# Joining 64-bit weights: the sign carried by ScalarE's slope instead of by a VectorE operation

## The chip, the cores and the metric

The kernel runs on one core of a Trainium2 chip. The metric is device time in microseconds (us), the median of three runs. Engines are named as the profile names them: PE is TensorE's matmul and PEld its weight load, DVE is VectorE, ACT is ScalarE, POOL is GpSimd, SP is the queue that issues most of the DMAs.

## The reference, cut to what matters

```python
# 8 x 8 heads of 576 tokens x 64; linear attention with two softmaxes
kv  = einsum('bhsd,bhse->bhde', softmax_over_tokens(k), v)
x   = einsum('bhsd,bhde->bhse', softmax_over_features(q), kv)   # 4608 tokens x 512
xn  = x / sqrt(mean(x * x) + 1e-6) * rms_g
x2  = (silu(xn @ w_gate) * (xn @ w_val)) @ w_out                # 512 -> 1536 -> 512
h   = maximum(maximum(x2 @ w1, x2 @ w2), x2 @ w3)               # 512 -> 768
out = h @ w2_out                                                # 768 -> 512
```

All weight matrices (`w_gate`, `w_val`, `w_out`, and `w1`, `w2`, `w3`, `w2_out` of the second layer) reach the chip as 64-bit floating-point numbers, seen as pairs of 32-bit words: a lower word and an upper word, alternating in memory.

## The kernel before, in words

The tokens are worked on in nine groups of 512 (`g` = 0 to 8). For each group the first layer runs over twelve blocks `f` of 128 hidden features. An iteration (g, f) multiplies the group's x by a gate block (12 matmuls into bank `pg`, L523 to L525), by a value block (12 into `pv`), forms tanh on ACT (L698), two products on DVE (L699, L710), splits the result into a high and a low part (L713 on ACT, L717 on DVE) and adds the block before it into the output (12 matmuls into `acc`, L529 to L531). There is one bank `pg`: L699 is its last reader, and the first matmul of the next iteration's gate product waits for it. Every matrix is held as a high and a low part of reduced width, so that each product takes three matmuls.

While group g is multiplied, the attention of group g + 1 is done between its iterations, in four pairs of heads: `k_max`, `k_exp`, `make_kv` (ten matmuls `pk`, L368), `make_x` (`px`) and so on. For group 1 (and 0) q is transposed on PE (`pt`, L388).

The weights of the first layer are built during group 0 alone, block f + 1 while block f is multiplied, in two halves of 768 columns (class `Weights`). One half goes through: load both words (SP), `scale` (L150: ACT multiplies the upper word, read as a 32-bit float, by 2^-112 into `y`), `join` (L155 to L157, three operations on DVE), `high` (L168, ACT) and `low` (L173, DVE). Block 0 and block 1 are built ahead of the first iterations, while the attention of group 0 is still running; group 0's scale `rstd` is found by a chain of small DVE operations (L458 to L474), goes through PE (L483) and ACT (L485), and is needed by `u` (L696), which for the first two blocks reads `pg` in place of L698 and L699.

The weights of the second layer are built during groups 1 to 7 (class `Ahead`), 24 pieces of 512 columns: load (SP), `join` (L213 on ACT, L214 to L216 on DVE, in place in tile `st`), sums (L228 to L231), and `quarter`, which splits on ACT and POOL and stores to memory. They are first read in group 8. From about 960 us on the second layer runs, and none of the joins is left.

No order of instructions is written out by hand. The framework places each engine's instructions in a queue by itself, from the order of the program and its own estimate of when operands will be there; each engine then works its queue strictly in that order. `tc.issue_after` ties a few helpers behind one instruction. In group 0 the joins of the two halves of a block stand mixed with the small operations of other chains on DVE, as the rows below show.

What a join before does, on integers: upper word scaled (its exponent field shrinks from 11 to 8 bits), shifted left by 3, then the sign taken from the original upper word, then the top 3 bits of the lower word put in at the bottom.

Of the kernel before, what the change touches and what calls it, by code (L numbers as in the profile page):

```python
# [8 lines left out]
F32 = mybir.dt.float32  # L9
F32R = mybir.dt.float32r  # L10
I32 = mybir.dt.int32
AF = mybir.ActivationFunctionType
ALU = mybir.AluOpType
# [34 lines left out]
def attention_moe_moe(ctx: ExitStack, tc: tile.TileContext, q, qt, k, kt, v, w1, rms_g, w2, w2_out, out):  # L48
# [14 lines left out]
    nc = tc.nc  # L63
# [60 lines left out]
    class Weights:  # L124
# [18 lines left out]
        def scale(self, f, h):  # L143
            if f in JOINED_IN:
                if h == 0:
                    self.place = wpool.tile([P, 2, HALF], F32, tag=JOINED_IN[f], name=f"y_{f}")
                self.y[f, h] = self.place[:, h, :]
            else:
                self.y[f, h] = two.tile([P, HALF], F32, tag="st", name=f"y_{f}_{h}")
            nc.scalar.activation(self.y[f, h], self.words[f, h][1].bitcast(F32), AF.Copy, scale=2.0**-112)  # L150

        def join(self, f, h):
            low, high = self.words.pop((f, h))
            y = self.y[f, h].bitcast(I32)
            nc.vector.tensor_scalar(y, y, 3, None, op0=ALU.logical_shift_left)  # L155
            nc.vector.scalar_tensor_tensor(y, high, -(2**31), y, op0=ALU.bitwise_and, op1=ALU.bitwise_or)
            nc.vector.scalar_tensor_tensor(y, low, 29, y, op0=ALU.logical_shift_right, op1=ALU.bitwise_or)  # L157

        def half(self, half, f, h):
            key = (1, f)  # L160
# [21 lines left out]
    class Ahead:  # L182
# [27 lines left out]

        def join(self, i):
            low, high = self.st[i]
            nc.scalar.activation(high.bitcast(F32), high.bitcast(F32), AF.Copy, scale=2.0**-112)  # L213
            nc.vector.tensor_scalar(low, low, 29, None, op0=ALU.logical_shift_right)  # L214
            nc.vector.scalar_tensor_tensor(low, high, -(2**31), low, op0=ALU.bitwise_and, op1=ALU.bitwise_or)
            nc.vector.scalar_tensor_tensor(high, high, 3, low, op0=ALU.logical_shift_left, op1=ALU.bitwise_or)  # L216

        def places(self, u):
# [314 lines left out]
    def evacuate(pt, dst, name, m, scale):  # L533
        pool, tag, bufs = ((two, "y", 3), (two, "y", 3), (two, "y", 3), (one, "sacc", 1))[m]
        e = pool.tile([P, N], F32, tag=tag, name=f"{name}_{m}", bufs=bufs)
        nc.scalar.activation(e, pt, AF.Copy, scale=scale)
        nc.scalar.dma_start(dst, e)
# [538 lines left out]
```

## Time and profile before

| | before |
|---|---|
| median of 3 runs | 1540.95 us (1540.77 to 1541.8) |
| profiled execution, its own time | 1538.84 us |
| span of the profile | 1537.0 us |
| PE busy | 1503.1 us (98%) |
| DVE busy | 939.8 us (61%) |
| ACT busy | 578.4 us (38%) |
| POOL busy | 259.1 us (17%) |
| mean granted clock of TensorE | 0.995 of full speed |

The span runs from the first to the last instruction; the profiled execution's own time is 1.84 us longer. Busy shares are means over stages that differ: group 0 lies between about 24 and 160 us, groups 1 to 8 end near 960 us, and the second layer takes the rest.

### The profile page before, as it was taken

What the parts mean: (1) busy time and instruction counts of PE and PEld (TensorE: products, weight loads), DVE (VectorE), ACT (ScalarE), POOL (GpSimd) and SP (SyncE); (2) the same over time, 40 slices, a digit from 0 to 9 for tenths busy, and PEclk for the clock granted to TensorE, in tenths of its full rate; (3) what the DMA queues carried; (4) which work ended last, traced back from release to release, by engine and by line L of the source; (5) the groups of instructions that cost most, each with busy time, mean ns of one, the idle gap of its engine ahead of it and who ended that gap; (6) DMA issues with size and microseconds to landing.
All of it is one profiled execution on the core that took longest, in us unless ns stands there. A gap on an engine that the chain in (4) does not pass through costs nothing.

```text
span 1537.0 us, 19169 instructions
## 1 busy us (share of the span) xinstructions
PE 1503.1 (98%) x6790; PEld 1238.1 (81%) x6790; DVE 939.8 (61%) x1622; ACT 578.4 (38%) x1107; POOL 259.1 (17%) x307
## 2 busy tenths in 40 slices
PE   5899999999999999999999999999999999999999
PEld 4678778888888888888888888888888888888887
DVE  6999655556655657655563244438838838847722
ACT  6764443433444434334433231323413413413311
POOL 0000222331331422312403200011111111111100
PEclk9999999999999999999999999999999999999999
DMA  8842552651652644626505113055485485485573
GB/s 274 324 157 73 166 136 94 172 149 57 195 163 68 192 135 130 176 91 181 172 29 171 49 55 124 0 181 209 163 315 207 170 321 199 168 299 198 171 265 104
DMA packets 126062, 250.00 MB, mean 163 GB/s; under 512 B 26640, under 2 KB 51216, under 8 KB 125968
## 3 DMA queue, kind: packets, MB, share of 16 engines
q1 hardware_dynamic: 119056, 236.21, 47.5%
q10 hardware_dynamic: 6912, 12.59, 2.2%
q8 instruction: 53, 0.87, 0.2%
q14 instruction: 41, 0.34, 0.1%
HBM read 205.52 MB, written 43.22 MB: 162 GB/s over the span
## 4 chain that ended last, share of the span: by engine, by line
PE 84%; DVE 8%; DMA 3%; issue 2%; POOL 1%; ACT 1%; SPq 0%; POOLq 0%; ACTq 0%; DVEq 0%
PE pg L523 6%; PE pg L525 5%; PE pg L524 5%; PE acc L529 5%; PE acc L530 5%; PE acc L531 5%; PE pv L523 5%; PE pv L524 5%; PE pv L525 5%; PE p_a L531 4%; PE p_a L530 4%; PE p_a L529 4%; PE p_G L529 2%; PE p_G L531 2%; PE p_G L530 2%; PE pk L368 2%
## 5 line engine op out<-in xcount | busy, mean ns | idle before, releaser
L699 DVE SCALAR_TENSOR_TENSOR t<-t,pg 128x512 f32<-128x512 f32 x106 | 72.3, 682 | 112.2 <-ACT t L698 110.3
L801 POOL TENSOR_TENSOR temps_wl<-temps_wh 128x512 f32<-128x512 f32 x36 | 48.2, 1338 | 438.2 <-ACT temps_wh L800 363.5
L713 ACT CAST hh<-t 128x512 fp32r<-128x512 f32 x108 | 66.9, 619 | 121.9 <-DVE t L710 121.1
L717 DVE TENSOR_TENSOR hl<-t,hh 128x512 fp32r<-128x512 f32 x108 | 77.4, 717 | 56.1 <-ACT hh L713 55.4
L710 DVE TENSOR_TENSOR t<-t,pv 128x512 f32<-128x512 f32 x108 | 73.9, 685 | 43.4 <-PE pv L525 40.0
L698 ACT ACTIVATE t<-pg 128x512 f32<-128x512 f32 x106 | 62.7, 591 | 88.6 <-PE pg L525 87.2
L529 PE MATMUL p_a<-x_wh,chunk 128*128 128x512 f32 x240 | 93.4, 389 | 0.0
L531 PE MATMUL p_a<-x_wh,chunk 128*128 128x512 f32 x240 | 93.4, 389 | 0.0
L530 PE MATMUL p_a<-x_wl,chunk 128*128 128x512 f32 x236 | 91.8, 389 | 0.0
L236 POOL TENSOR_TENSOR wq<-st,wq 128x256 fp32r<-128x256 f32 x84 | 64.2, 779 | 39.0 <-ACT wq L235 34.3
L336 POOL TENSOR_TENSOR q<-q,qm 128x512 f32<-128x512 f32 x28 | 30.3, 1083 | 209.7 <-DVE qm L326 178.5
L796 ACT COPY temps_wh<-p_G 128x512 f32<-128x512 f32 x36 | 21.1, 586 | 104.5 <-PE p_G L531 104.2
L310 POOL TENSOR_TENSOR qT<-qT,stat 128x512 f32<-128x512 f32 x28 | 37.5, 1340 | 132.3 <-DMA stat<-stats 132.3
L93 DVE TENSOR_TENSOR ql<-qT,qh 128x512 fp32r<-128x512 f32 x24 | 18.5, 770 | 58.6 <-ACT qh L92 58.3
L427 POOL TENSOR_TENSOR sacc<-sacc,sq 128x512 f32<-128x512 f32 x21 | 27.4, 1303 | 159.3 <-ACT sq L426 135.6
L529 PEld LDWEIGHTS p_a<-x_wh,chunk 128*128 128x128 f32 x240 | 45.1, 188 | 9.3
L531 PEld LDWEIGHTS p_a<-x_wh,chunk 128*128 128x128 f32 x240 | 45.1, 188 | 9.3
L530 PEld LDWEIGHTS p_a<-x_wl,chunk 128*128 128x128 f32 x236 | 44.3, 188 | 9.2
L529 PE MATMUL p_G<-x_wh,chunk 128*128 128x512 f32 x123 | 48.2, 392 | 0.2
L531 PE MATMUL p_G<-x_wh,chunk 128*128 128x512 f32 x123 | 47.9, 389 | 0.0
L337 ACT ACTIVATE q<-q 128x512 f32<-128x512 f32 x28 | 17.7, 632 | 75.1 <-POOL q L336 67.4
L798 DVE TENSOR_TENSOR temps_wh<-temps_wh,p_V 128x512 f32<-128x512 f32 x36 | 24.6, 683 | 33.4 <-PE p_V L531 33.4
(689 smaller groups left out, 4523.3 us busy)
## 6 DMA issues: line engine op xcount, KB each, us to landing
chunk<-w_dram SPq DMA_DIRECT2D x112, 768.0 KB, 4.4
w_dram<-wq SPq DMA_DIRECT2D x84, 256.0 KB, 3.0
words<-in_w SPq DMA_DIRECT2D x24, 768.0 KB, 7.9
stat<-stats SPq DMA_DIRECT2D x112, 128.0 KB, 3.2
chunk<-w_dram SPq DMA_DIRECT2D x48, 256.0 KB, 3.6
k<-in_k SPq DMA_DIRECT2D x30, 320.0 KB, 4.0
v<-in_v SPq DMA_DIRECT2D x30, 320.0 KB, 4.5
st<-in_w SPq DMA_DIRECT2D x18, 512.0 KB, 4.8
```

Of the source, the lines that this page charges most:

```text
L236: nc.gpsimd.tensor_sub(t[:, 1, :], src, t[:, 0, :].bitcast(F32))
L523: nc.tensor.matmul(pt, hi[:, j, s], xhs[kk], start=(kk == 0), stop=False)
L524: nc.tensor.matmul(pt, hi[:, j, s], xls[kk], start=False, stop=False)
L525: nc.tensor.matmul(pt, lo[:, j, s], xhs[kk], start=False, stop=(kk == 3))
L529: nc.tensor.matmul(pt, ah, bh, start=first, stop=False, skip_group_check=onto)
L530: nc.tensor.matmul(pt, ah, bl, start=False, stop=False, skip_group_check=onto)
L531: nc.tensor.matmul(pt, al, bh, start=False, stop=last, skip_group_check=onto)
L698: nc.scalar.activation(t, pg, AF.Tanh, scale=0.5)
L699: nc.vector.scalar_tensor_tensor(t, t, 1.0, pg, op0=ALU.add, op1=ALU.mult)
L710: nc.vector.tensor_mul(t, t, pv)
L713: nc.scalar.copy(hh[g, f], t)
L717: lows.append(nc.vector.tensor_sub(hl[g, f], t, hh[g, f].bitcast(F32)))
```

## The change: what it does

ACT's scaling becomes a parametric ReLU: positive values are multiplied by 2^-112 as before, negative ones by 2^-112 times 2^32. For a negative word the factor of 2^32 adds 32 to the exponent field, which sets a bit that the shift left by 3 moves into the place of the sign. So the DVE operation that put the sign back is left out in both classes. In `Weights.join` the shift that stood alone now works on the lower word, in place, and the shift of `y` moves into the last operation; in `Ahead.join` the two operations that are left are the same as before.

```diff
-            nc.scalar.activation(self.y[f, h], self.words[f, h][1].bitcast(F32), AF.Copy, scale=2.0**-112)
+            nc.scalar.activation(self.y[f, h], self.words[f, h][1].bitcast(F32), AF.Prelu, scale=2.0**-112, alpha=2.0**32)
 
         def join(self, f, h):
-            low, high = self.words.pop((f, h))
+            low, _ = self.words.pop((f, h))
             y = self.y[f, h].bitcast(I32)
-            nc.vector.tensor_scalar(y, y, 3, None, op0=ALU.logical_shift_left)
-            nc.vector.scalar_tensor_tensor(y, high, -(2**31), y, op0=ALU.bitwise_and, op1=ALU.bitwise_or)
-            nc.vector.scalar_tensor_tensor(y, low, 29, y, op0=ALU.logical_shift_right, op1=ALU.bitwise_or)
+            nc.vector.tensor_scalar(low, low, 29, None, op0=ALU.logical_shift_right)
+            nc.vector.scalar_tensor_tensor(y, y, 3, low, op0=ALU.logical_shift_left, op1=ALU.bitwise_or)
...
         def join(self, i):
             low, high = self.st[i]
-            nc.scalar.activation(high.bitcast(F32), high.bitcast(F32), AF.Copy, scale=2.0**-112)
+            nc.scalar.activation(high.bitcast(F32), high.bitcast(F32), AF.Prelu, scale=2.0**-112, alpha=2.0**32)
             nc.vector.tensor_scalar(low, low, 29, None, op0=ALU.logical_shift_right)
-            nc.vector.scalar_tensor_tensor(low, high, -(2**31), low, op0=ALU.bitwise_and, op1=ALU.bitwise_or)
             nc.vector.scalar_tensor_tensor(high, high, 3, low, op0=ALU.logical_shift_left, op1=ALU.bitwise_or)
```

## Rows read from the trace of the kernel before

**Rows 1.** Page, part 1: busy us of each engine, share of span, instructions.
```profile
PE 1503.1 (98%) x6790; PEld 1238.1 (81%) x6790; DVE 939.8 (61%) x1622; ACT 578.4 (38%) x1107; POOL 259.1 (17%) x307
```

**Rows 2.** Windows: stretch, length, busy us (instructions) per engine, TensorE clock, DMA share, GB/s.
```profile
24.00:52.00 28.00, 18.34 (x81) 12.59 (x81) 25.02 (x54) 19.31 (x42) 0.00 (x0) 0.81 0.78 284
52.00:112.00 60.00, 59.59 (x268) 47.31 (x269) 58.92 (x101) 41.47 (x98) 0.62 (x6) 0.98 0.63 218
112.00:152.00 40.00, 39.28 (x181) 31.69 (x180) 39.59 (x70) 19.18 (x28) 0.20 (x2) 1.00 0.22 64
...
164.00:310.00 146.00, 141.53 (x647) 115.45 (x646) 84.28 (x159) 58.65 (x110) 39.92 (x49) 1.00 0.49 143
310.00:840.00 530.00, 529.77 (x2440) 440.36 (x2439) 310.13 (x576) 215.99 (x404) 145.68 (x175) 1.00 0.47 138
```

**Rows 3.** PE timeline, 29 to 52 us: start, length, instruction, [idle before it, releaser].
```profile
30.23 2.52 PE L368 MATMUL pk<-wh,wh 128*128 128x129 f32 x10 [0.35 <-DVE kv_raw L378]
...
48.52 1.11 PE L483 MATMUL rstd<-ident,z 128*128 128x128 f32 x4 [5.59 <-DVE z L474]
```

**Rows 4.** DVE timeline, 23 to 52 us.
```profile
25.66 0.96 DVE L156 SCALAR_TENSOR_TENSOR y<-words,y 128x768 int32<-128x768 int32 x1
...
41.65 0.95 DVE L156 SCALAR_TENSOR_TENSOR y<-words,y 128x768 int32<-128x768 int32 x1
...
48.39 0.95 DVE L156 SCALAR_TENSOR_TENSOR y<-words,y 128x768 int32<-128x768 int32 x1
49.26 1.81 DVE L157 SCALAR_TENSOR_TENSOR y<-words,y 128x768 int32<-128x768 int32 x2
50.99 0.68 DVE L696 TENSOR_TENSOR u<-pg,z 128x512 f32<-128x512 f32 x1
```

**Rows 5.** Waits of PE, whole span: who waited for whom, us in total, times, longest.
```profile
PE pg L523 <- DVE t L699: 2.6, 6, 0.8
```

**Rows 6.** DVE groups by form: count, busy us, mean ns of one, idle before.
```profile
L156 DVE SCALAR_TENSOR_TENSOR y<-words,y 128x768 int32<-128x768 int32 x24 | 22.7, 951 | 0.1
...
L215 DVE SCALAR_TENSOR_TENSOR st<-st 128x512 int32<-128x512 int32 x24 | 18.1, 755 | 2.6 <-ACT st L213 1.7 <-DVE ks L372 0.4
...
L155 DVE TENSOR_SCALAR y<-y 128x768 int32<-128x768 int32 x24 | 13.1, 552 | 0.7 <-ACT y L150 0.6
L214 DVE TENSOR_SCALAR st<-st 128x512 int32<-128x512 int32 x24 | 10.1, 423 | 22.6 <-DMA st<-in_w 19.7 <-DMA st<-in_w_out 2.9
...
L495 DVE TENSOR_SCALAR z<-var 128x512 int32<-128x512 int32 x7 | 3.0, 424 | 9.7 <-ACT var L493 9.7
```

**Rows 7.** ACT groups by form: count, busy us, mean ns of one, idle before.
```profile
L698 ACT ACTIVATE t<-pg 128x512 f32<-128x512 f32 x106 | 62.7, 591 | 88.6 <-PE pg L525 87.2 <-DVE hl L717 1.3
...
L150 ACT ACTIVATE y<-words 128x768 f32<-128x768 f32 x24 | 21.2, 907 | 3.9 <-DMA words<-in_w 2.2 <-DVE wl_(1, 4)_825 L173 0.8 <-DVE wl_(1, 10)_1348 L173 0.7
...
L420 ACT COPY xraw<-px 128x512 f32<-128x512 f32 x32 | 18.7, 585 | 16.4 <-PE px L410 8.2 <-PE px L404 7.2 <-PE px L406 0.8
...
L333 ACT ACT_TABLE_LOAD x1 | 1.3, 1283 | 4.8 <-DMA q<-in_q 4.8
...
L416 ACT ACTIVATE xraw<-px,gain 128x512 f32<-128x512 f32 x4 | 2.7, 683 | 4.3 <-PE px L406 4.3
```

**Rows 8.** PE timeline in group 0: transposes and `pk` of pairs two and four.
```profile
81.27 0.60 PE L388 MATMUL pt<-ident,q 128*128 128x128 f32 x4
81.70 1.28 PE L368 MATMUL pk<-v,k 128*128 128x129 f32 x10
...
121.70 1.28 PE L368 MATMUL pk<-v,k 128*128 128x129 f32 x10
```

**Rows 9.** Chain that ended last, group 2: start, us, what.
```profile
324.28 1.11 PE pk L368 x10
342.58 1.11 PE pk L368 x10
```

**Rows 10.** DVE timeline, 301 to 308 us, ahead of a late L699.
```profile
304.54 1.67 DVE L216 SCALAR_TENSOR_TENSOR st<-st 128x512 int32<-128x512 int32 x1
```

## The prediction, written before the changed kernel was run

> **What bounds the kernel now.** The page's busy shares come first [rows 1]: PE is busy for 98% of the span and DVE for 61%. Read alone, that says that DVE's time is worth nothing. The windows [rows 2] say where this fails. From 310 us to 840 us PE is busy for 529.77 of 530 us, so there nothing on another engine matters. Between 24 and 152 us, the stretch in which the first layer's weights are joined, DVE is busy for 25.02 + 58.92 + 39.59 = 123.5 of 128 us. There DVE is the full engine, and from 24 to 52 us PE is busy for only 18.34 of 28 us, at a mean granted clock of 0.81, so partly at the lower of TensorE's two levels (1.2 and 2.4 GHz). From 164 to 310 us PE misses 146 - 141.53 = 4.5 us.
>
> The PE timeline shows the largest pause of all [rows 3]: 5.59 us before the matmul of L483, which waits for the last L474, the end of the small chain that finds group 0's scale. The DVE timeline shows what that chain stands behind [rows 4]: joins are queued between its small steps, among them L156. After it comes `u` (L696), at 50.99 us, again behind an L156 and two L157. The waits of PE add one thing for later [rows 5]: the gate product waited for L699 six times, 2.6 us in all.
>
> **The change part by part.** *Removed.* 24 L156, 951 ns each, 22.7 us, and 24 L215, 755 ns each, 18.1 us, both on DVE [rows 6]. In a full queue one costs less than its length, since the next starts before it ends: L156 at 48.39, L157 at 49.26, so 0.87 us [rows 4]. DVE's busy time should fall from 939.8 to about 899 us.
>
> *Rewritten.* L155 now works on the lower word, which lies with a gap of one word. No row has that at 768 columns. L214 does it at 512 in 423 ns and L155 takes 552 ns without gaps [rows 6]; 423 + 256 x (552 - 423)/256 is the same 552, so I take no change. The bounds are 423 ns from below and the 951 ns of a two-operand form from above, that is -3 to +10 us of DVE time in all. It also no longer waits for ACT, because it reads the lower word alone. The last operation keeps its form and inputs of the same kind, so 951 ns.
>
> *ACT.* No row has a parametric ReLU. L150 takes 907 ns with a plain copy. From PSUM, a tanh (L698) takes 591 ns where a copy (L420) takes 585 ns, and a copy whose scale is read from memory (L416) takes 683 ns [rows 7]. So a join costs ACT between 0 and 98 ns more; nothing in the rows gives a gain. I take 6 ns, the change of function alone, since slope and scale are constants: 48 x 6 = 0.3 us, at most 48 x 98 = 4.7 us of ACT, of which only the few joins on the chain reach the end. ACT is busy for 80 of the 128 us between 24 and 152 us [rows 2]; if it had no room, that 2.4 us (24 x 98 ns) would be lost.
>
> The profile holds one table load on ACT, 1283 ns, though exp, tanh, square and copy all run [rows 7]. The Trainium skill, "ScalarE: Activation LUTs", section "Table sets: the hidden batching unit", says that functions are loaded in named sets, that relu, copy, identity and abs are in every set, and that a switch costs about 2.66 us; parametric ReLU is not in its list. The load of 1283 ns agrees with the page's own figure; no row shows whether parametric ReLU is in the set that is loaded. If it is, the sum below stands; if not, the last rival's does.
>
> *Term A, 24 to 52 us.* The chain here passes through L156 five times, but not all of that comes back. The first joins stand beside a PE at the low clock: `pk` at 30.23 waited 0.35 us for DVE [rows 3], so I give this part 0.4 us. The chain behind it has three L156 left: at 41.65, one of the same kind at 47.45, and at 48.39 [rows 4]. Two delay L474 and so L483, the third, with the L157 behind it, delays `u`. 3 x 0.87 = 2.6. A = 0.4 + 2.6 = 3.0 us. At least the two in front of L483 come back, 1.7 us; at most the five of the chain, and L155 leaving the chain once, 5 x 0.87 + 0.55 = 4.9 us.
>
> *Term B, 52 to 152 us.* 18 L156 fall here, 15.7 us of DVE, but PE is already nearly full, so only PE's losses can come back. Two measures of these. Matmuls per time: 530 us hold 2440 later on, 0.217 us each; 268 and 181 of them would take 58.2 and 39.3 us and take 60 and 40, a loss of 2.5 us [rows 2]. Time per pair: in group 0 from 81.70 to 121.70, 20.0 us, of which four transposes take 0.43 [rows 8]; in group 2 it takes 18.30 [rows 9]. So a pair loses 20.0 - 0.43 - 18.30 = 1.27 us, and 100 us lose 6.4. The truth is between, since the matmuls differ in kind. What is late next is PE itself, at its own pace. DVE keeps 58.92 + 39.59 - 15.7 = 82.8 of 100 us, so the greater part should return: B = 3.5 us, with 1 and 6.4 as ends. Low clock (0.98 here) makes up some: 0.02 x 60 = 1.2 us, and comes back only if the pause before it becomes short enough.
>
> *Term C, 152 us on.* Of the six waits for L699, four have L215 and L216 directly ahead of it in DVE's queue (the one at 304.54 stands for them [rows 10]). Each loses one operation of about 0.6 us from start to start, and no wait was longer than 0.8 us. 4 x 0.6 = 2.4; two waits are themselves shorter than 0.6 us, so C = 2.2 us, from 0.5 to 3. From 310 us on the joins are hidden under PE; after 840 us nothing changes. No DMA moves to another place; a tile comes free earlier by the operation left out, and the words' next load starts that much earlier, into a DMA share of 0.63 and 0.22 [rows 2].
>
> Sum: 3.0 + 3.5 + 2.2 = 8.7 us. The profiled execution took 1538.84 us (span 1537.0 and 1.84 around it), so 1530.1; its own span would be 1528.3. The median of the runs lies 2.1 us above the profiled execution, which gives **1532.2 us**.
>
> **The rivals.**
>
> *PE is the bound and takes nothing.* DVE's saved time becomes idle time, because the framework plans its queue anew with shorter joins and puts other work into the gaps. For it: PE is at 98%, and the losses in B are spread thin. Against it: three L156 lie plainly on the chain before 52 us. Then only A's lower end is left, or less: a gain of 0 to 3 us, say 1539.5 us.
>
> *The new queue order puts joins in front of L699.* The queue's order is the framework's, and what is ahead of L699 when the gate product has ended makes PE wait. At 304.54 L216 takes 1.67 us and L699 can only follow [rows 10]; it goes away with L215 only if the two do not meet elsewhere. Now there are six such waits in 28 pair boundaries of groups 1 to 7. At 0.8 us each, the longest of them [rows 5], A and B (6.5 us) are eaten when 8 more boundaries wait; from 12 more on the kernel is slower by over 0.2%. With 16 more, the time is 1540.95 - 6.5 + 12.8 = 1547 us. Against it: 22 of 28 boundaries already hold with more joins in the queue.
>
> *Parametric ReLU is not in the loaded set.* Then each join swaps the table twice, 2 x 1.283 = 2.57 us of ACT [rows 7]. In group 0, 24 joins add 62 us to ACT's 80 in a stretch of 128: ACT becomes the bound and the stretch grows by at least 14 us. The later 24 would each hold L698 for up to 2.57 us; at 1 us on PE each, 24 more. 1541 + 38 = 1579 us. This is the skill's rule named above, priced from rows. For it there is no row; against it, that four functions share one load.
>
> **How the numbers follow.** Forecast 0.75 (its own range 1527 to 1538), the first rival 0.16, the second 0.06, the last 0.03. What a measurement of this kernel can tell from no change is about 0.2%, 3.1 us. The forecast's low end is the sum of the upper ends, 4.9 + 6.4 + 3 = 14.3 us: 1526.7. Its high end with A, B and C at their lower ends, 3.2 us, is 1537.7, just outside no change. The range runs from 1527 to 1541, into the first rival, and leaves out the others. Faster 0.75, within 0.2% 0.16, slower 0.09.
>
> **What would show it.** In the changed profile L156 and L215 are gone, DVE's busy time is near 899 us, L150 stays within 0.91 to 1.01 us, and there is one table load. The pause before L483 is about 3.9 us instead of 5.59, `u` starts near 48 us, the last `pk` of group 0 comes 5 to 7 us earlier than 121.70, and DVE is clearly below nine tenths from 52 to 152 us. In group 1 the waits of PE for L699 fall from 2.6 to below 1 us. The forecast is wrong if `u` starts at 50 us or later, if group 0 ends less than 3 us earlier, if the waits for L699 in groups 1 to 7 grow, or if more than one table load appears.

## The result, and the profile after

The changed kernel takes **1526.43 us** (median of four runs, 1524.64 to 1528.49) beside 1541.38 us for the kernel before in the same session: ratio 0.9903, interval 0.9886 to 0.9920. A repeat in a later session gives 1530.51 beside 1543.13 us, ratio 0.9914 (0.9897 to 0.9931). So it is faster by 0.9%, between 12.6 and 15 us. The profiled execution took 1528.49 us against 1538.84 before, 10.35 us less; its span is 1526.3 us.

The page, part 1, of the kernel after: busy us, share of the span, instructions.
```profile
PE 1502.8 (98%) x6790; PEld 1241.5 (81%) x6790; DVE 907.8 (59%) x1574; ACT 578.5 (38%) x1107; POOL 259.6 (17%) x307
```
Against [rows 1] DVE has 48 instructions less and 32.0 us less, not the 41 us forecast. PE has the same work and, but for 0.3 us, the same busy time: the shorter span comes from PE standing still for 23.5 us instead of 33.9.

The groups by form, on DVE and ACT (count, busy us, mean ns of one, idle before). In the kernel after, L155 shifts the lower word, L156 is the last operation of the first layer's join, L213 and L214 are the second layer's two; from there on line numbers are lower by one or two than before.
```profile
L156 DVE SCALAR_TENSOR_TENSOR y<-y,words 128x768 int32<-128x768 int32 x24 | 22.7, 948 | 0.9 <-ACT y L150 0.8
L155 DVE TENSOR_SCALAR words<-words 128x768 int32<-128x768 int32 x24 | 13.1, 556 | 0.2
...
L214 DVE SCALAR_TENSOR_TENSOR st<-st 128x512 int32<-128x512 int32 x24 | 18.5, 773 | 3.1 <-ACT st L212 2.5
L213 DVE TENSOR_SCALAR st<-st 128x512 int32<-128x512 int32 x24 | 10.2, 424 | 22.4 <-DMA st<-in_w 19.1 <-DMA st<-in_w_out 3.3
```
```profile
L150 ACT ACTIVATE y<-words 128x768 f32<-128x768 f32 x24 | 21.4, 912 | 2.4 <-issue 1.2 <-DVE wl_(1, 5)_922 L172 0.6 <-DVE wl_(1, 10)_1326 L172 0.5
...
L331 ACT ACT_TABLE_LOAD x1 | 1.3, 1283 | 4.5 <-DMA q<-in_q 4.5
```
The shift of the gapped lower word costs 556 ns where the shift without gaps took 552, the parametric ReLU 912 ns where the copy took 907 [rows 6, 7], and there is still one table load.

The windows of the kernel after (stretch, length, busy us and instructions per engine, TensorE clock, DMA share, GB/s); after them one stretch of the kernel before.
```profile
24.00:52.00 28.00, 24.00 (x90) 18.23 (x89) 21.29 (x49) 19.11 (x42) 0.00 (x0) 0.70 0.74 273
52.00:112.00 60.00, 58.90 (x278) 47.96 (x277) 58.93 (x104) 45.98 (x105) 0.62 (x6) 1.00 0.65 234
112.00:152.00 40.00, 40.00 (x189) 33.08 (x188) 34.07 (x65) 19.84 (x29) 0.21 (x2) 1.00 0.23 71
152.00:290.00 138.00, 137.68 (x631) 113.43 (x630) 76.98 (x144) 56.08 (x106) 38.37 (x47) 1.00 0.50 148
...
310.00:840.00 530.00, 530.00 (x2447) 440.45 (x2446) 298.48 (x551) 214.51 (x400) 143.89 (x171) 1.00 0.46 135
```
```profile
152.00:290.00 138.00, 133.78 (x610) 109.05 (x609) 81.71 (x153) 56.55 (x106) 34.99 (x45) 1.00 0.47 139
```
Read the instruction counts, not the busy shares alone. From 52 to 112 us PE is busy for less than in [rows 2] (58.90 against 59.59 us) and does ten matmuls more, at a granted clock of 1.00 instead of 0.98. DVE stays full there (58.93 of 60 us), because joins of later blocks move into this stretch: it holds 13 last operations of a join (L156) and 14 subtractions (L172), where before it held ten of each (L157, L173). The largest difference stands where the forecast had put the least: from 152 to 290 us PE is busy for 137.68 instead of 133.78 us.

PE's timeline around the matmul of group 0's scale (start, length, instruction, idle before it), and below it the pair that answers to 121.70 in [rows 8].
```profile
44.87 0.39 PE L523 MATMUL pv<-raws,wl_(1, 0)_455 128*128 128x512 f32 x1
45.31 0.65 PE L481 MATMUL rstd<-ident,z 128*128 128x128 f32 x4
46.64 0.32 PE L355 MATMUL pb<-ident,km 128*128 128x128 f32 x1 [0.68 <-ACT z L483]
48.12 0.64 PE L521 MATMUL pg<-raws,wh_(1, 1)_523 128*128 128x512 f32 x1 [1.16 <-DVE u L694]
...
116.50 1.28 PE L366 MATMUL pk<-v,k 128*128 128x129 f32 x10
```
DVE's timeline ahead of it, and below it two rows of the kernel before, in which the chain that finds the scale reads its sums (L458, L456 after) and ends (L474, L472 after):
```profile
36.48 0.95 DVE L156 SCALAR_TENSOR_TENSOR y<-y,words 128x768 int32<-128x768 int32 x1
...
41.99 0.83 DVE L456 TENSOR_SCALAR var<-pv 128x1 f32<-128x1 f32 x4 [3.27 <-PE pv L442]
...
45.10 0.16 DVE L472 SCALAR_TENSOR_TENSOR z<-a,z 128x4 f32<-128x4 f32 x1
45.18 0.55 DVE L155 TENSOR_SCALAR words<-words 128x768 int32<-128x768 int32 x1
45.65 1.82 DVE L172 TENSOR_TENSOR wl_(1, 1)_545<-y,wh_(1, 1)_523 128x768 fp32r<-128x768 f32 x2
47.38 0.68 DVE L694 TENSOR_TENSOR u<-pg,z 128x512 f32<-128x512 f32 x1
```
```profile
40.45 0.35 DVE L458 TENSOR_SCALAR var<-pv 128x1 f32<-128x1 f32 x4
...
48.31 0.15 DVE L474 SCALAR_TENSOR_TENSOR z<-a,z 128x4 f32<-128x4 f32 x1
```
The 5.59 us pause of [rows 3] is gone, but only 3.2 us of that is the scale's matmul coming earlier (45.31 instead of 48.52). The rest is that the gate and value matmuls of block 0, which before had ended at 42.9 us, now run until 45.3. The chain itself has a new order: it begins 1.5 us later than before and takes 3.1 us from its first row to its last instead of 7.9, because the joins that stood between its steps [rows 4] now stand ahead of it or behind it. `u` starts at 47.38 instead of 50.99 [rows 4], with one shift and two subtractions between it and the scale, and no L156. Group 0's last `pk` comes 5.20 us earlier.

The waits of PE after, from 24 to 152 us, and below them all that it waited for from 152 to 290 us; the third fence is that last stretch of the kernel before (who waited for whom, us in total, times, longest).
```profile
PE pg L521 <- DVE u L694: 1.2, 1, 1.2
PE pg L521 <- ACT wh_(1, 3)_717 L167: 1.1, 1, 1.1
...
```
```profile
PE pg L521 <- DVE t L697: 0.2, 1, 0.2
```
```profile
PE pg L523 <- DVE t L699: 2.1, 4, 0.8
PE px L408 <- ACT kvh L92: 2.1, 2, 1.4
```
Up to 152 us the change brings one new wait, 1.1 us for block 3's upper half, and `u` still holds up 1.2 us. From 152 us on, before, the four waits of [rows 5] that fall into this stretch take 2.1 us, and the two for `kvh` another 2.1. After, 0.2 us are left of it all.

Two marks divide the rest: the `pk` of a pair at the start of group 1's stretch (mark 1) and the one four pairs later (mark 2), here before and then after.
```profile
174.34 1.28 PE L368 MATMUL pk<-v,k 128*128 128x129 f32 x10
287.04 1.27 PE L368 MATMUL pk<-v,k 128*128 128x129 f32 x10
```
```profile
169.07 1.27 PE L366 MATMUL pk<-v,k 128*128 128x129 f32 x10
276.71 1.28 PE L366 MATMUL pk<-v,k 128*128 128x129 f32 x10
```
From mark 1 to mark 2 it is 112.70 us before and 107.64 after. By these marks the profiled executions differ as follows: 3.61 us up to `u`, 1.59 more up to group 0's last `pk`, 0.07 more to mark 1, 5.06 in group 1, and 0.4 behind it (the last matmul starts at 1532.95 and at 1522.23).

### The profile page after: what moved, and what is told of

Its sections match the earlier page's. It is cut to its first block, busy times and chain, and to the rows that moved or that the text cites. A ratio compares the mean times of both kernels' runs of the same rounds, so it can differ in the third digit from the quotient of the medians.

```text
span 1526.3 us, 19104 instructions
## 1 busy us (share of the span) xinstructions
PE 1502.8 (98%) x6790; PEld 1241.5 (81%) x6790; DVE 907.8 (59%) x1574; ACT 578.5 (38%) x1107; POOL 259.6 (17%) x307
## 4 chain that ended last, share of the span: by engine, by line
PE 94%; DVE 2%; ACT 1%; DMA 1%; POOL 1%; issue 1%; SPq 0%; POOLq 0%; ACTq 0%; DVEq 0%
PE pg L521 7%; PE pg L523 6%; PE pg L522 6%; PE acc L527 6%; PE pv L523 6%; PE acc L528 6%; PE pv L521 6%; PE pv L522 6%; PE acc L529 6%; PE p_a L528 4%; PE p_a L527 4%; PE p_a L529 4%; PE p_G L527 2%; PE p_G L528 2%; PE p_G L529 2%; PE pk L366 2%
## 5 line engine op out<-in xcount | busy, mean ns | idle before, releaser
L335 ACT ACTIVATE q<-q 128x512 f32<-128x512 f32 x28 | 17.7, 633 | 76.8 <-POOL q L334 70.9
L233 ACT CAST wq<-st 128x256 fp32r<-128x256 f32 x84 | 33.6, 418 | 32.1 <-DMA w_dram<-wq 17.1
```

## The experiments

Each was timed in five rounds against the kernel before. "Stretch" is the time from mark 1 to mark 2.

**The change again.** No edit.

> The changed kernel once more, for the interval and for a second profile. Theory 'clock': the 4.2 us by which its median lies closer to a gain of 15 us than its profiled execution does (10.35 us) is TensorE at its lower clock between 24 and 52 us in some executions and not in others; then executions of the changed kernel differ by 2 to 4 us, the longer ones have the lower mean clock, and a profile of a short one (about 1524.5 us) shows a granted clock near 0.9 or more in 24 to 52 us where the first profile shows 0.70. Rival 'constant offset': every execution takes the same time up to 0.5 us, and the profile is only slower by its recording; then the new profile shows 0.70 there again and the times stay apart.

Measured: 1530.51 us, ratio 0.9914. The repeat's profile has `u` 2.16 us earlier than before, mark 1 3.93, mark 2 9.57 and the last matmul 8.28 us. So the parts repeat: the start gives 2 to 4 us, group 1 gives 5 to 6. What is behind mark 2 doesn't: 0.4 us more was won there, 1.3 us are given back here. Runs of the same kernel differ: before took 1538.14 to 1548.20 us over these sessions, and the six runs of this repeat 1525.19 to 1532.18, so the rival of a constant offset falls. Whether the clock makes the difference stays open: the execution that was profiled was the longest of the six (granted clock 0.76 from 24 to 52 us), and no short one was.

**The first layer's joins alone.**
```diff
 class Weights:   # scale: Prelu, join: two operations, as in the change
 class Ahead:     # scale: Copy, join: three operations, as before
```


> Only the first layer's weights are joined in the new way; the second layer's joins stay as before. Theory 'operations': terms A and B come with it and C does not: about 5.3 us less in the profile (3.6 up to u and 1.7 up to the last pk of group 0), and PE's waits in group 1 stay at 2 us or more. Rival 'order': the gain of group 1 comes from a queue order that group 0's shorter work brings about; then about 10 us less, with POOL's q subtraction of group 1 no longer behind the weight splits.

Measured: 1532.92 us, ratio 0.9937 (0.9921 to 0.9953). That is the size that the rival had given (about 10 us), not the theory's 5.3, and the stretch is 108.48 us. What the rival named as the reason isn't there, though: POOL's subtraction for q (L335, at 171.44 us) still stands behind weight splits.

**The second layer's joins alone.** The same edit the other way round.

> Only the second layer's weights are joined in the new way. Theory 'operations': term C alone, 2.2 us as predicted, up to the 5.4 us that the profile of the changed kernel shows after 152 us; nothing before 152 us. Rival 'order': 0 to 2 us, and the pause of PE near 183 us, behind POOL's weight splits, stays.

Measured: 1540.67 us, ratio 0.9984 (0.9975 to 0.9993). The parts are 9.7 and 2.5 us by ratio, together 12.2 beside 13.3 for the whole in the same session. The second layer's part is what term C gave it, but it isn't where C put it: its stretch is 112.40 us, as before, although L215 is gone; with L215 kept and the first layer's joins new it is 108.48 us. One profile of this kernel doesn't show where its 2.5 us lie. A place that fits is the time behind mark 2, which [rows 5] make look empty. From 290 us on PE waits for DVE and ACT for nothing in this profile; in the nine profiles of kernels that keep L215 it waits 0.5 to 3.7 us (0.5 in the kernel before), in the five of kernels without it 0 to 2.1 us. The two ranges overlap, so this isn't shown.

**The steeper slope alone.** The scaling as in the change; every operation of VectorE is kept.
```diff
-nc.scalar.activation(..., AF.Copy, scale=2.0**-112)
+nc.scalar.activation(..., AF.Prelu, scale=2.0**-112, alpha=2.0**32)
```


> ACT's parametric ReLU in both places, and all VectorE operations as before (the sign is then put in twice, which changes nothing). Theory: no change, within 1 us, L150 at 0.91 us, one table load, the same order on every queue. Rival: the framework's estimate of the new function differs and so does its order; then several us either way with the same busy times.

Measured: 1544.07 us, ratio 1.0005 (0.9995 to 1.0015). L150 takes 903 ns here, and there is one table load:
```profile
L333 ACT ACT_TABLE_LOAD x1 | 1.3, 1283 | 4.7 <-DMA q<-in_q 4.7
```
The function costs nothing that this run can tell from none, and the rival of the swapped tables falls. The Trainium skill, "ScalarE: Activation LUTs", section "Table sets: the hidden batching unit", doesn't list parametric ReLU among what every set holds; this trace shows it running beside exp and tanh under one load.

**Blocks 0 to 2 alone, and blocks 3 to 11 alone.** The change made for a part of the first layer's blocks; the second layer as before.
```diff
+if f <= 2:      # in the other kernel: f >= 3
+    Prelu, two operations
+else:
+    Copy, three operations
```


> New join for blocks 0 to 2 of the first layer only; blocks 3 to 11 and the second layer as before. It separates term A. Theory 'backlog' (DVE falls behind in group 0, its late joins run into group 1's first q chain, and the 5 us of group 1 come from their being done earlier): u 3.0 to 3.6 us earlier, but the backlog is only shifted, so block 11 is still joined near 150 us, the second layer's first two pieces are still loaded after the last join, and PE's waits in group 1 stay; 3 to 4 us in all. Rival 'start' (a start earlier by 3 us is what moves group 1): 8 us or more in all.

> New join for blocks 3 to 11 of the first layer only. Theory 'backlog': u where it was before, block 11 joined near 130 us, the second layer's first loads 20 us earlier, PE's waits in group 1 below 1 us in place of 4.7 (2.6 for L699 and 2.1 for kvh): 5 to 7 us in all. Rival 'start': at most 2 us, with group 1 as before.

Measured: blocks 0 to 2 give 1541.38 us, ratio 0.9986 (0.9978 to 0.9995), 2.2 us; blocks 3 to 11 give 1535.61 us, ratio 0.9951 (0.9938 to 0.9964), 7.6 us. With the early blocks `u` comes 4.62 us sooner than before, more than in the whole change, and most of it is given back at once: 1.78 us are left at group 0's last `pk`. The windows and PE's waits of this kernel from 52 to 112 us:
```profile
52.00:112.00 60.00, 56.25 (x257) 43.99 (x255) 59.32 (x101) 41.81 (x98) 0.62 (x6) 1.00 0.62 227
```
```profile
PE pg L530 <- ACT wh_(1, 3)_718 L175: 2.2, 1, 2.2
PE pv L530 <- DVE t L717: 1.1, 2, 0.8
```
(Line numbers here are higher by eight or nine than in the kernel after.) DVE is full for 59.32 of 60 us, so a PE that arrives earlier waits for block 3's weights. In group 1 little is won (stretch 111.92 us). With the late blocks it is the other way: `u` stays late (+1.09 us), and the stretch falls to 107.65 us. So the rival 'start' falls in both; the theory's sizes (3 to 4 and 5 to 7 us) were missed by 0.8 and 0.6 us.

**The second layer's first joins held back,** in the kernel after, until block 11's `hl` is subtracted.
```diff
+with tc.issue_after(lows[-2].ins) if (g, f) == (1, 0) else ExitStack():
     second.advance(f)
```
**The second layer's first unit left out of DVE,** in the kernel before. It leaves out the first two pieces' DVE joins and the sums made from them; ScalarE fills their places with copies.
```diff
 def join(self, i):
+    if i < 2:
+        # two copies on ScalarE
+        return
 def sums(self, u):
+    if u == 0:
+        return
```


> The changed kernel, with the DVE operations of the second layer's first unit (two joins and four sums) tied behind the last split of group 0, so that they run where they ran in the kernel before. Theory 'backlog': q's statistics of group 1 are late again and PE waits again; 2 to 5 us of the gain are lost against the changed kernel, all between the first and the last pk of group 1. Rival 'order on POOL or ACT alone': within 1 us of the changed kernel.

> The kernel before, without the DVE part of the second layer's first unit: the two joins' DVE operations and the sums are left out, and ACT fills the lower words by a copy of 0.68 us each, so the values of this unit are not the reference's. Theory 'backlog': group 0 as before, and 3 to 5 us less in group 1, since nothing stands in q's chain any more. Rival: at most the DVE time itself, under 1 us, as DVE is idle for half of group 1.

Measured: holding back gives 1530.24 us, ratio 0.9920 (0.9907 to 0.9933), not to be told from the change itself; but only part of the work moved (the second piece was still joined at 136 us), so it is a weak test. Leaving out gives 1541.85 us, ratio 0.9990 (0.9979 to 1.0001), with a stretch of 113.28 us and 4.3 us of PE's waits for L699 and `kvh` in group 1 (4.2 in the kernel before). The theory had forecast 2 to 5 us lost and 3 to 5 us won; neither came. So the waits of group 1 don't come from the second layer's first joins that stand among group 1's small operations.

**Blocks 10 and 11 alone, blocks 3 to 9 alone, a delay, and the removal without the rewriting.** The first two are the edit above with `f >= 10` and `3 <= f <= 9`. The third is the kernel after with
```diff
+if nxt == 1:
+    z = rstd[nxt][1].bitcast(I32)
+    for _ in range(8):
+        nc.vector.tensor_scalar(z, z, -1, None, op0=ALU.bitwise_and)
 if nxt not in COMPACT:
     newton_step(nxt, 2)
```
The fourth is the kernel before with Prelu in `Weights` and its sign operation left out, the two others as they were.

> The kernel before, with the new join for blocks 10 and 11 alone (4 of the 18 joins of blocks 3 to 11). The late-blocks run took 5.1 us less of PE waiting in group 1 (152 to 290 us) than the kernel before. Theory 'boundary' (VectorE comes to the end of group 0 with block 11's joins still in its queue, and they stand ahead of group 1's scale and normalise work; what is late there stays late through group 1): these four joins are the ones that stand there, so most of the 5.1 us goes: 3 to 5 us between 152 and 290 us, block 11's last subtraction done by about 146 us or earlier against 152.3, ratio about 0.9965 to 0.998. Rival 'sum of backlog' (each lighter join of blocks 3 to 11 gives its share, since VectorE has been behind since block 3): 4/18 of it, about 1.1 us in group 1, ratio about 0.999. Theory of the prediction's step C (the waits of group 1 come from the second layer's joins, whose instructions are as before here): 0 in group 1, ratio 0.9995 to 1.0.

> The kernel before, with the new join for blocks 3 to 9 alone (14 of 18 joins). 'Boundary': the backlog that stands there at the end of group 0 is what decides, and blocks 10 and 11 keep their three operations; VectorE still arrives earlier by what the 14 joins leave of it; if its backlog is caught up in each block, then 0 to 2 us in group 1, ratio 0.998 to 0.9995. 'Sum of backlog': 14/18 of it, about 4 us in group 1 and 1.5 us before it, ratio about 0.9962. With e9 the two parts add to the late-blocks run (0.9951) if the shares are additive; if one of them alone already gives 4 us of group 1, the waits have a threshold.

> The kernel after, with eight more operations of VectorE (each a pass over 128x512 words that leaves them as they are, by the shift of the same size about 0.55 us, so about 4.4 us together) just ahead of group 1's third Newton step and its normalise operations. 'Boundary': VectorE's lead of about 4 us at the end of group 0 is gone, so the waits of group 1 that the change took come back: 3 to 6 us between 152 and 290 us, ratio to the kernel before about 0.9935 to 0.995. 'The first unit of the second layer, or VectorE's lighter load inside group 1, gives the gain': group 1 stays as in the kernel after but for a single wait of TensorE of at most 4.4 us less its slack; ratio 0.9905 to 0.992 if that wait is hidden.

> The kernel before, with the steeper slope and the first layer's sign operation left out, but the other two operations as they were (the shift of the scaled word stays first and waits for ScalarE; the fold of the lower word stays second); the second layer's joins as before. Against the run with the first layer's joins new (0.9937) it tells what the rewriting of the two operations that are left adds to leaving one out. Theory of the prediction (the sum counts one operation less and the shift no longer behind ScalarE): leaving out carries all but about 1 us: ratio about 0.9940 to 0.9950. Rival (it is the shift's wait for ScalarE that put blocks 1 to 3 and 11 late): the gain is halved, ratio about 0.9965 to 0.998.

Measured: blocks 10 and 11 give 1542.11 us, ratio 0.9991 (0.9981 to 1.0001); blocks 3 to 9 give 1535.66 us, ratio 0.9945 (0.9928 to 0.9962); the delay gives 1534.26 us, ratio 0.9941 (0.9927 to 0.9954); the removal alone gives 1530.89 us, ratio 0.9923 (0.9908 to 0.9938).

The first form of the boundary theory, that block 11's own joins are what stands in the way, fell: its four joins take 1.0 us off group 1. Blocks 3 to 9 alone take off all of it, with a stretch of 107.34 us. The rival 'sum of backlog' had given 1.1 us for the first and 4 for the second; they took off 1.0 and 5.4, together more than the 5.05 of the late-blocks kernel, so the shares don't add. The theory that remains is that what counts is how late DVE as a whole is when group 1 begins. The delay shows that from the other side. Its DVE timeline (the eight added operations, then group 1's normalise and the reciprocal of the next q; line numbers behind the edit are higher by four), PE's marks, PE's waits between 152 and 290 us, and the window with the lower clock:
```profile
143.87 3.20 DVE L679 TENSOR_SCALAR z<-z 128x512 int32<-128x512 int32 x7 [1.71 <-ACT z L483]
...
147.58 0.42 DVE L679 TENSOR_SCALAR z<-z 128x512 int32<-128x512 int32 x1
148.04 2.74 DVE L508 SCALAR_TENSOR_TENSOR xraw<-xraw,gain,z 128x512 f32<-128x512 f32 x4
...
159.32 0.20 DVE L305 RECIPROCAL qr<-qs 128x8 f32<-128x8 f32 x1
```
```profile
167.81 1.28 PE L366 MATMUL pk<-v,k 128*128 128x129 f32 x10
280.75 1.28 PE L366 MATMUL pk<-v,k 128*128 128x129 f32 x10
```
```profile
PE pg L521 <- DVE t L701: 2.0, 3, 1.0
PE px L406 <- ACT kvh L92: 0.9, 1, 0.9
PE pk L366 <- issue: 0.5, 1, 0.5
```
```profile
196.00:204.00 8.00, 6.35 (x21) 4.44 (x20) 6.39 (x17) 3.88 (x7) 1.07 (x4) 0.79 0.60 148
```
The added work is 3.6 us of DVE (the expectation had reckoned 4.4). Against PE's mark 1, DVE's normalise moves from 23.85 us ahead (169.07 - 145.22) to 19.77. The same two kinds of wait come back, 2.9 us, and the stretch is 112.94 us, 5.3 more than in the kernel after; the boundary theory had forecast 3 to 6. About 1.7 us of that is the granted clock, 0.79 over 8 us, in the window that holds two of the waits. By ratio the delay costs 4 to 6 us against the change (0.9941 beside 0.9914 and 0.9903); its interval, 0.9927 to 0.9954, just touches that of the repeat and not that of the first measurement.

All kernels, by the same marks. "Lead" is mark 1 less the start of the reciprocal of the next group's first q (`qr`, L307 before, L305 after), so how far DVE is ahead of PE. Lead and stretch are from one profile each; only the changed kernel has two:

| kernel | `qr` | mark 1 | lead | stretch | ratio |
|---|---|---|---|---|---|
| before | 168.51 | 174.34 | 5.8 | 112.7 | 1 |
| early blocks | 166.74 | 172.57 | 5.8 | 111.9 | 0.9986 |
| slope alone | 169.62 | 175.44 | 5.8 | 113.6 | 1.0005 |
| second layer alone | 167.25 | 174.99 | 7.7 | 112.4 | 0.9984 |
| after, with delay | 159.32 | 167.81 | 8.5 | 112.9 | 0.9941 |
| first unit left out | 166.8 | 175.57 | 8.8 | 113.3 | 0.9990 |
| blocks 10 and 11 | 165.38 | 174.46 | 9.1 | 111.7 | 0.9991 |
| after, joins held | 158.6 | 169.58 | 11.0 | 108.3 | 0.9920 |
| late blocks | 160.6 | 172.80 | 12.2 | 107.7 | 0.9951 |
| blocks 3 to 9 | 159.43 | 171.62 | 12.2 | 107.3 | 0.9945 |
| first layer alone | 157.09 | 169.28 | 12.2 | 108.5 | 0.9937 |
| removal alone | 156.9 | 169.12 | 12.2 | 106.5 | 0.9923 |
| after | 156.88 | 169.07 | 12.2 | 107.6 | 0.9903 |
| after, again | 158.2 | 170.41 | 12.2 | 107.1 | 0.9914 |

With a lead of 11 to 12 us the stretch is 106.5 to 108.5 us, with 9.1 or less it is 111.7 to 113.6; no kernel lies between. In the kernel after the lead can't grow further, because there the q chain waits for ScalarE and not for DVE's queue:
```profile
155.96 0.69 DVE L302 TENSOR_REDUCE qs<-q 128x8 f32<-128x512 f32 x1 [1.98 <-ACT q L335]
```
In the kernel before, DVE comes to the normalise only behind block 11's last subtraction:
```profile
151.31 0.95 DVE L173 TENSOR_TENSOR wl_(1, 11)_1429<-y,wh_(1, 11)_1407 128x768 fp32r<-128x768 f32 x1
153.44 2.74 DVE L510 SCALAR_TENSOR_TENSOR xraw<-xraw,gain,z 128x512 f32<-128x512 f32 x4 [1.18 <-ACT z L485]
```
After, that last subtraction comes at 129.89 us and the normalise at 145.22.

How the lateness reaches PE shows at the first wait for L699 in group 1, in the kernel before (POOL's row first, then DVE's):
```profile
182.55 1.04 POOL L336 TENSOR_TENSOR q<-q,qm 128x512 f32<-128x512 f32 x1
```
```profile
184.29 0.69 DVE L304 TENSOR_REDUCE qs<-q 128x8 f32<-128x512 f32 x1 [1.99 <-ACT q L337]
...
185.53 0.69 DVE L699 SCALAR_TENSOR_TENSOR t<-t,pg 128x512 f32<-128x512 f32 x1
```
The next q goes from POOL (L336) through ACT (L337) to DVE (L304), L699 stands behind it in DVE's queue, and no join is between them. In each run the framework also plans POOL's and ACT's queues anew, so their order is a rival. In this stretch it isn't the cause by itself: POOL's order (two operations on `qT`, four splits, then the subtraction) is the same in the kernel after, with the delay and with blocks 10 and 11, and the last two have the waits. No run moves DVE's lead while every queue keeps its order.

The removal without the rewriting gives as much as the first layer's part with it (0.9923 and 0.9937, the intervals overlap; the expectation had 0.9940 to 0.9950). So the gain of the first layer's joins is the operation left out; that the shift no longer waits for ScalarE adds nothing that shows.

## Why the prediction was right or wrong, point by point

The direction was right, and so was the bound: DVE was the full engine of group 0. The forecast was 1532.2 us with a range from 1527 to 1541. The runs gave 1526.4, just below its low end, and the repeat 1530.5, inside it; on which side the median fell is in part luck.

What failed is a step of the mechanism. Terms B and C cut the gain apart at 152 us: B let "only PE's losses" up to 152 us come back, and C gave all that comes later to L215 and L216, at most 3 us. The runs showed in its place that DVE's lateness from group 0 is handed on: group 1 gave 5.06 us (5.64 in the repeat), and 4.22 us of that come with the first layer's joins alone, L215 kept.

- **Costs of the operations: right.** 556 ns for the gapped shift (taken: 552), 948 for the last operation (951), 912 for the scaling (913), one table load.
- **Term A, taken as 3.0 us: right in size, in part by luck.** `u` is 3.6 us earlier, 2.2 in the repeat, and group 0's last `pk` 5.2 (forecast: 5 to 7), 3.9 in the repeat. The chain behind `pk` had the three L156 that were named, but they didn't just drop out of it: with the new order the chain became 4.8 us shorter and began 1.5 us later, and the pause before the scale's matmul, forecast at about 3.9 us, is gone. The removal without the rewriting comes nearer to the forecast's picture: a pause of 3.36 us, and `u` 3.1 us earlier. And A alone isn't kept: with blocks 0 to 2 alone `u` gains 4.6 us and the kernel 2.2, since a full DVE gives PE the difference back as a wait for block 3.
- **Term B, taken as 3.5 us up to 152 us: too large at its place, too small as a cause.** 1.6 us come back between `u` and group 0's last `pk`. "Only PE's losses can come back" was counted up to 152 us alone. The joins of blocks 3 to 11, from which B was made, are worth 7.6 us by the median, and of the 6.6 us by which their profile is ahead at mark 2, 5.1 are won behind mark 1: DVE's lateness is handed on.
- **Term C, taken as 2.2 us (0.5 to 3): its cause was wrong.** The waits of [rows 5] were put down to L215 and L216, which stand directly ahead of L699 in the queue [rows 10]. That reading was too wide: of the six waits (0.43, 0.45, 0.43, 0.82, 0.24 and 0.23 us), the first and the third have q's sums and no join ahead of L699, the second has second-layer sums and q's sums in between, and the four that were counted are together 1.7 us long, not 2.4. Without L215 alone they stay (stretch 112.40 us). With L215 kept and the first layer's joins new, the stretch is 108.48 us, though a few waits of up to 0.8 us remain. The place was right, the waits fell from 2.6 to 0.2 us (1.1 in the repeat), and those for `kvh` went with them; group 1 gave 5.1 us, outside the bounds. That the joins are hidden under PE from 310 us on was read from one profile; in others of kernels that keep L215 PE misses up to 3.9 us between 290 and 830 us.
- **"DVE clearly below nine tenths from 52 to 152 us": wrong.** 58.93 + 34.07 of 100 us is 93%. Its busy time fell by 32.0 us, not 41. The means of all forms times their counts add up to 1011.9 us before and 973.0 after, 38.9 less; the page's busy time, which counts overlapping operations once, falls by less, since in a full queue one starts before the last has ended. The forecast used this (0.87 us) for the chain but not for the sum.
- **From the profile to the median: the larger part of the miss.** The sum gave 1530.1 us for a profiled execution, and that took 1528.49: 1.6 us. The forecast added 2.1 us, because before's median lay above its profiled execution; after's lies 2.06 us below. That is 4.2 of the 5.8 us. One execution's distance from the median is a draw from a spread of several us, not a property that the next kernel inherits.
- **Rivals.** "PE takes nothing" fell, and so did the table swap. "The new order puts joins in front of L699" didn't come: 0.2 us of such waits, 1.1 in the repeat; the new order showed at the start instead, in the chain of the scale.

What stays open is how much of group 1's gain is DVE's lead and how much the order of the other queues, which changed with it. Single executions also differ behind mark 2 while the medians agree (against the kernel before 5.4 us lost with blocks 10 and 11, 4.3 with the slope alone); part of this is waits for L699, 3.3 and 2.1 us behind 290 us in these two profiles and 0.5 in the kernel before. Why they come in one execution and not in another isn't known.

## What to carry to other kernels

A queue that is full in one stage can send the bill to the next: when you price work taken out of a full engine, follow what it delivers late into the next stage, and count the waits there too. What stands directly ahead of a waiting instruction isn't yet the cause of the wait; ask how late the whole queue was when it got there, and test that by a delay of known length. Forecast a median from several runs' median, not from one profiled execution and its distance to it.

## What the runs showed of the hardware that was not expected

- PE's busy time fell where it did more: 58.90 us for 278 matmuls at a granted clock of 1.00, against 59.59 us for 268 at 0.98. From 24 to 52 us it is the reverse: 24.00 us busy at 0.70 against 18.34 us at 0.81, for 9 matmuls more. Part of the longer busy time is matmuls at the lower level of 1.2 GHz (0.63 us for one of 512 columns at 48.56 us, 0.39 us at 44.87).
- A slope of 2^32 on the negative side has no cost that can be told from none: the pass over 768 columns takes 912 ns in the kernel after and 903 with the slope alone, where the plain copy takes 907.
- The gain of group 1 came nearly as a step: 1.9 to 3.3 us more lead than before changed the stretch by between -1.0 and +0.6 us (second layer alone, first unit left out, blocks 10 and 11), 5.1 us shortened it by 4.4, and 6.4 us by 4.2 to 6.2.
